# Attention forward and backward with a gated feed-forward block on one core: GpSimd's loads in program order, each tied to its own slot

## The chip, the core and the metric

The kernel runs on one core of a Trainium2 chip. The metric is the device time of one execution in microseconds (us); less is better. A core has five engines that run their own instruction streams: PE (TensorE), DVE (VectorE), ACT (ScalarE), POOL (GpSimd) and SP (SyncE). POOL and SP mostly issue transfers here, and the core's 16 DMA engines carry them. A GB/s is 10^9 bytes per second; a KB is 1024 bytes.

## The reference

From x (2048 x 576) comes xn = layernorm(x). Attention with 32 heads of width 128 takes its keys and values (2048 each) from caches; a second branch is a gated feed-forward block of inner width 4608. The output and the gradients for x, both caches and all weights are returned.

```python
xn = layernorm(x)
q = (xn @ wq) as 32 heads of 128
p = softmax(q @ k_cache^T * 128**-0.5)
s = (p @ v_cache, heads joined) @ wo
h = sigmoid(xn @ w_gate) * (xn @ w_up)
g = silu(h @ w_down)
out = x + s * g
# returned: out, and the gradients of A_x, A_k_cache, A_v_cache, A_wq, A_wo, B_w_gate, B_w_up, B_w_down for grad_out
```

## The kernel before

The work runs in stages: the feed-forward block forward (until about 490 us), attention forward and backward in one pass over the heads (490 to 3680 us), a first late stage that multiplies the heads' outputs by wo (3680 to 3830 us), and late stages for the remaining gradients.

*Attention* (function `attention(fast)`, L562). It is built twice, and a flag chooses the fast one, which is the one that ran. Its plan is written in slots, 2 x 16 for each of the 32 heads. In the first 16 slots of head h (from b1 = 32 h) the slot's `main1` makes a tile of 128 query rows: scores on PE (L600), exponential on ACT into a slab `Pq` of 128 x 2048 (L618), and a transpose of the slab by DMA from SP's queue (L594, `PT`). I call this the softmax phase. In the next 16 (from b2 = b1 + 16), the dp phase, `main2` makes dp = dO V^T on PE (L670) and multiplies it into the slab on DVE, the first half by way of ACT (L677, L678), the second half directly (L673); then the slab is transposed by DMA again (`dST`). Each slab is 512 KB, so each slot moves 512 KB through a DMA transpose. Five slots later (`skew`) the transposed tile is multiplied on PE (`tail1` with Vn, `tail2` with Kn, both L647), and every fourth slot a group of o or dq is stored by POOL (L641). The sums over queries for dV and dK (`Partial`, L706) run spread over eight slots each; every four steps L718 on DVE puts the result into a tile `kvo`, of which there are two buffers, and POOL stores it (L720): four stores of dV in the first half of the dp phase, four of dK in the first half of the next softmax phase.

*Other units of a slot.* `put(slot, cols, fn)` adds a unit of work to a slot; `plan(h)` puts all units of head h. For the next head it puts the loads of K and V in four parts of 128 KB (L178), wo (L172, L174) and wq (L164, L166), and their preparation: `prep_kt` (K transposed on PE, slot b2 + 8 of the head before), `prep_wot` and the four `prep_qt` (from b2 + 9), `prep_vt` (slot b1 + 6 of its own head). K and wq have two sets of buffers, V and wo one.

*Order.* In this stage no engine is held to the order in which the code is written: the Tile scheduler orders each engine's instructions, and a load goes into POOL's queue about as soon as its buffer is free. So the four V loads leave together when the last `tail1` of a head is done, and the four K loads when the last `tail2` of the head before is done. Each queue then runs in the order that was fixed: an instruction of POOL that waits holds up all behind it.

*Last head.* For the first late stage all of A_wo (4.7 MB) is loaded into buffers that the last head no longer needs (`wo_parts`, L535; `load_wo_rows`, L544), in parts of up to four heads (576 KB).

*First late stage* (from L860). For each of 16 row tiles, 32 x 2 matmuls (L902) multiply a transposed o tile `oT` (1 MB, DMA transpose from SP, L554; three buffers, loaded two tiles ahead) with wo. Then DVE combines the result with `dsg`, `g2b` and `xb`, which POOL loads for groups of SG1 = 2 tiles (288 KB each, L876), one group ahead, in two buffers each; POOL stores `xb` after each group (L912). SP and POOL are in program order there.

Of the kernel before, what the change touches and what calls it, by code (L numbers as in the profile page):

```python
# [9 lines left out]
bf = mybir.dt.bfloat16  # L10
# [3 lines left out]
P = 128  # L14
# [52 lines left out]
def kernel(  # L67
# [112 lines left out]
    def load_k(hs, c=0, n=1):  # L180
        load_kv(hs, hs.Kn, A_k_cache, c, n)
# [377 lines left out]
    NSC = S // CH  # L559
    nb = CH // P  # L560

    def attention(fast):  # L562
        with ExitStack() as es:
            def pool(name, bufs, **kw):
                return es.enter_context(tc.tile_pool(name=("f_" if fast else "g_") + name, bufs=bufs, **kw))
            slabp = pool("slab", SLABS)
# [123 lines left out]
            class Partial:  # L690
# [9 lines left out]
                def step(self):  # L700
                    kt = self.kt
                    j = kt % 4
                    if j == 0:
                        self.tile = acc_tile()
                    for qt in range(self.lo, self.hi):
                        nc.tensor.matmul(self.tile[:, j, :], lhsT=self.slabs[qt][:, kt * P:(kt + 1) * P], rhs=self.rhs[:, qt, :],  # L706
                                         start=(qt == self.lo), stop=(qt == self.hi - 1))
                    self.kt += 1
                    if j == 3 or self.kt == NT:
                        k0 = kt - j  # L710
                        if self.out_dram is None:
                            if self.factor == 1.0:
                                alt.copy(self.part[:, k0:kt + 1, :], self.tile[:, :j + 1, :], eng=self.eng)
                            else:
                                alt.scaled(self.part[:, k0:kt + 1, :], self.tile[:, :j + 1, :], self.factor, eng=self.eng)
                        else:
                            fo_ = stg.tile([P, 4, P], bf, name="kvo")
                            nc.vector.scalar_tensor_tensor(fo_[:, :j + 1, :], self.tile[:, :j + 1, :], self.factor, self.part[:, k0:kt + 1, :],  # L718
                                                           op0=ALU.mult, op1=ALU.add)
                            nc.gpsimd.dma_start(self.out_dram.rearrange("(p t) d -> p t d", t=NT)[:, k0:kt + 1, :], fo_[:, :j + 1, :])  # L720
# [7 lines left out]
            def put(slot, cols, fn):  # L728
                units.setdefault(slot, []).append((cols, fn))
# [18 lines left out]
            def q(k):  # L748
                return min(k, NT - 1)

            def plan(h):
                b1, b2 = 2 * NT * h, 2 * NT * h + NT
                hd = lambda: heads[h]
                pl = b2 - 2 * NT if h else None
                if h:
                    put(pl, 0, lambda: heads.__setitem__(h, start_head(h)))
                    for c in range(4):
                        put(pl + q(c), 0, lambda c=c: load_k(hd(), c, 4))
                        put(pl + q(skew + 3 + c), 0, lambda c=c: load_v(hd(), c, 4))
                    put(pl + q(4), 0, lambda: load_wo(hd()))  # L760
                    put(pl + q(5), 0, lambda: load_wq(hd()))
                    put(pl + q(skew + 3), NT * P, lambda: prep_kt(hd()))
                    put(pl + q(skew + 4), DT * P, lambda: prep_wot(hd()))
                    for sc in range(NSC):
                        put(pl + q(skew + 4 + 2 * sc), DT * CH, lambda sc=sc: prep_qt(hd(), sc))
                for qt in range(NT):
                    put(b1 + qt + skew, NT * P // 2, lambda qt=qt: tail1(hd(), qt, 0))
                    put(b1 + qt + skew, NT * P // 2, lambda qt=qt: tail1(hd(), qt, 1))
                for sc in range(NSC):
                    put(b1 + q(sc), DT * CH, lambda sc=sc: prep_dot(hd(), sc))  # L770
                    put(b1 + q(sc + 1), nb * P, lambda sc=sc: prep_don(hd(), sc))
                for qt in range(NT):
                    put(b1 + max(qt + 1, q(2 + qt // nb)), 0, lambda qt=qt: scale_don(hd(), qt))
                put(b1 + q(NSC + 2), NT * P, lambda: prep_vt(hd()))
                put(b1 + q(NTH + 2), NT * P, lambda: prep_qn(hd()))
                for qt in range(NT):
                    put(max(b1 + qt + 1, b1 + NT - 4 + qt // 2), 0, lambda qt=qt: scale_qn(hd(), qt))
                put(b2 + 1, 0, lambda: post1(hd()))
                parts = {}

                def first(key, rhs, lo, hi, eng, factor=1.0):
                    parts[key] = part_tile()
                    return Partial(hd(), lo, hi, rhs, parts[key], None, eng, factor)
                spread(b1 + NTH, lambda: first("v", hd().dOn, 0, NTH, "v"))
                spread(b2, lambda: Partial(hd(), NTH, NT, hd().dOn, parts["v"], out_3[0, h], None))
                spread(b2 + NTH, lambda: first("k", hd().Qn, 0, NTH, "s", SCALE))
                spread(b2 + NT, lambda: Partial(hd(), NTH, NT, hd().Qn, parts["k"], out_2[0, h], None, SCALE))
                for qt in range(NT):
                    put(b2 + qt + skew, NT * P // 2, lambda qt=qt: tail2(hd(), qt, 0))
                    put(b2 + qt + skew, NT * P // 2, lambda qt=qt: tail2(hd(), qt, 1))  # L790

            heads[0] = start_head(0)
            for h in range(H):
                plan(h)
            bl = 2 * NT * (H - 1) + NT
            for view, h0, n, dead in wo_parts:
                for k in range(0, n, 4):
                    at = (1 + k // 4, q(skew + 1), q(skew + 2), q(skew + 4), q(skew + 5))[dead]
                    put(bl + q(at), 0, lambda view=view, h0=h0, k=k, n=n: load_wo_rows(view, h0, k, min(k + 4, n)))
            for st in range(min(2, NT)):  # L800
                put(bl + NT + skew * st, 0, lambda st=st: load_oT(oTs[st], st))
            slot = 0
# [32 lines left out]
    with late("pc") as pc, late("pcw") as pcw, late("pcf") as pcf, \  # L835
# [21 lines left out]
                if i == DT - 1 and KPAD:  # L857
                    nc.gpsimd.memset(wdT_sb[:LO, i, r0:r0 + WCH], 0.0)

        with late("c1l3", 2) as ldp3, late("c1s", 2) as sb, \  # L860
                late("c1ps", 2, space=PSUM) as ps, late("c1pt", 2, space=PSUM) as pst:
            wo_of = {}
            for view, h0, n, _ in wo_parts:
# [2 lines left out]
            oTs.append(oT_view(xn_all[:].rearrange("p t d -> p (t d)"), 0))  # L866
            if NT > 2:
                load_oT(oTs[2], 2)
            SG1 = ldiv(NT, 2)
            NG1 = NT // SG1  # L870

            def group_loads(g):
# [4 lines left out]
                    res.append(t_)  # L877
                return res

            groups = {0: group_loads(0)}  # L880
            pend_tr = []
            for st in range(NT):
                if st and st + 2 < NT:
                    load_oT(oTs[(st + 2) % 3], st + 2)
                g, sl = divmod(st, SG1)
                if sl == 0:
                    if g + 1 < NG1:
                        groups[g + 1] = group_loads(g + 1)
                    dsg, g2b, xb = groups.pop(g)
                if st >= NT - 2 - DT and len(wd_pieces) > (F // WCH - 1) * DT:  # L890
                    wd_piece()
                if st == NT - NT // 4:
                    load_blk(ah0[:, 0, :, :], a_d, 0)
                    load_blk(ah0[:, 1, :, :], h_d, 0)
                while len(pend_tr) > 1:
                    st_ = pend_tr.pop(0)
                    transpose_to(nc, pst, doB[:, st_, :], D, doBT, st_ * P, ident, alt, eng="s")
                oT = oTs[st % 3]
                accs = [ps.tile([P, 512], f32, name=f"acc{j}") for j in range(len(ncs))]
                for h in range(H):  # L900
                    for j, (n0, nn) in enumerate(ncs):
                        nc.tensor.matmul(accs[j][:, :nn], lhsT=oT[:, h, :], rhs=wo_of[h][:, n0:n0 + nn],  # L902
                                         start=(h == 0), stop=(h == H - 1))
                s_sb = sb.tile([P, D], f32, name="s_sb")
                for j, (n0, nn) in enumerate(ncs):
                    alt.copy(s_sb[:, n0:n0 + nn], accs[j][:, :nn], eng="s")
                nc.vector.tensor_tensor(doB[:, st, :], s_sb[:], dsg[:, sl, :], op=ALU.mult)
                t0 = sb.tile([P, D], f32, name="t0")
                nc.vector.tensor_tensor(t0[:], s_sb[:], g2b[:, sl, :], op=ALU.mult)
                nc.vector.tensor_tensor(xb[:, sl, :], t0[:], xb[:, sl, :], op=ALU.add)  # L910
                if sl == SG1 - 1:
                    nc.gpsimd.dma_start(o0[g * SG1 * P:(g + 1) * SG1 * P, :].rearrange("(t p) d -> p t d", p=P), xb[:])  # L912
                pend_tr.append(st)
# [263 lines left out]
```

## Time and profile before

| what | value |
|---|---|
| three runs, median | 5086.49 us |
| lowest and highest of them | 5072.76 and 5111.36 us |
| the profiled execution: its own time | 5090.96 us |
| span of its instructions | 5089.0 us |
| mean granted TensorE clock | 0.993 |
| DMA issues of K and V parts | 128 KB, median 3.2 and 5.0 us to landing |
| DMA issues of dV and dK (kvo) | x256, 128 KB, median 4.2 us to landing |
| DMA transposes PT and dST | x512 each, median 4.9 and 5.2 us to landing |

A page of the profile gives each engine's busy time and its share of the span, then the chain of work that ended last, traced back from the last instruction: at each step to what released it. "issue" in it is time in which an engine waited for nothing that the profile shows. Groups and waits are named by line, engine and tiles (out<-in). A "landing" is the time from the issue of a transfer until its semaphore tells that it is done. DMA share is the mean busy share of the 16 DMA engines; it can exceed 1, since the packets of two queues overlap in the record.

### The profile page before, as it was taken

Reading aid. Unit: us, or ns where it says so; the run is one execution under the profiler, and the core shown is the slowest. Engines: PE = TensorE matmul, PEld = TensorE weight load, DVE = VectorE, ACT = ScalarE, POOL = GpSimd, SP = SyncE. Lnnn points to the kernel's source line nnn. Section 1 sums busy time; section 2 is a strip of 40 time slices with the busy share of each in tenths; the row PEclk is TensorE's granted clock in tenths of the full one; section 3 lists DMA queues with packets and bytes.
Section 4 is the critical chain, followed back from the end, with each engine's and each line's share of the span. In section 5 each row is a group of like instructions: output and inputs, shape, how many; then the busy total and the mean of one; then the engine's idle time right before and its main releaser. Section 6 shows DMA issues by size and latency. Waiting matters only on the chain.

```text
span 5089.0 us, 128042 instructions
## 1 busy us (share of the span) xinstructions
PE 4934.5 (97%) x53584; PEld 3485.5 (68%) x54480; DVE 2582.2 (51%) x6705; ACT 2577.3 (51%) x4636; POOL 938.9 (18%) x1449
## 2 busy tenths in 40 slices
PE   8999999999999999999999999999889999999999
PEld 4445777777787777778777777877646666555554
DVE  4544666666566666566666665666525444200111
ACT  5422666666676666667666666766413333211000
POOL 3322111111111111111111111111112222211000
PEclk9999999999999999999999999999999999999999
DMA  7776999999999999999999999999996665797976
GB/s 266 262 201 167 210 198 208 205 212 202 197 212 212 205 208 203 199 202 212 210 205 202 203 214 202 211 207 201 215 197 203 190 185 181 217 265 181 173 141 121
DMA packets 2762161, 1031.37 MB, mean 203 GB/s; under 512 B 2664737, under 2 KB 2668962, under 8 KB 2761570
## 3 DMA queue, kind: packets, MB, share of 16 engines
q1 hardware_dynamic: 2660354, 699.97, 74.0%
q0 software_dynamic: 101216, 323.05, 20.0%
q8 instruction: 428, 7.01, 0.6%
q14 instruction: 163, 1.34, 0.1%
HBM read 175.31 MB, written 182.13 MB: 70 GB/s over the span
## 4 chain that ended last, share of the span: by engine, by line
PE 83%; issue 8%; DMA 5%; DVE 1%; POOL 1%; ACT 1%; SPq 0%; POOLq 0%; DVEq 0%; ACTq 0%
PE acc L706 15%; PE acc L647 15%; PE acc L932 13%; PE sp L600 7%; PE acc L1103 7%; PE acc L213 5%; PE dp L670 5%; PE u_ps L420 3%; PE g_ps L418 3%; PE dh L985 3%; PE acct L146 2%; PE acc L503 2%; DMA out_dram<-kvo 2%; PE acc L902 2%; DVE Pq L673 1%
## 5 line engine op out<-in xcount | busy, mean ns | idle before, releaser
L618 ACT ACTIVATE Pq<-sp 128x1024 bf16<-128x1024 f32 x1024 | 1047.9, 1024 | 315.5 <-PE sp L600 202.1
L706 PEld LDWEIGHTS <-Pq 128*128 128x128 bf16 x16384 | 1006.9, 98 | 242.7 <-issue 5.0
L677 ACT ACTIVATE t<-dp,negdelta 128x1024 bf16<-128x1024 f32 x512 | 571.6, 1116 | 224.0 <-PE dp L670 170.6
L673 DVE SCALAR_TENSOR_TENSOR Pq<-dp,negdelta,Pq 128x1024 bf16<-128x1024 f32 x512 | 655.0, 1279 | 43.9 <-PE acc L647 41.1
L647 PEld LDWEIGHTS <-PT 128*128 128x128 bf16 x8192 | 503.1, 98 | 133.8 <-DMA PT<-Pq 13.3
L670 PE MATMUL dp<-VT,dOT 128*128 128x512 bf16 x1728 | 544.2, 382 | 36.6 <-DVE Pq L673 36.5
L647 PE MATMUL acc<-Vn,PT 128*128 128x128 bf16 x8192 | 548.3, 219 | 18.5 <-DMA PT<-Pq 11.6
L647 PE MATMUL acc<-Kn,dST 128*128 128x128 bf16 x8192 | 552.3, 219 | 8.5 <-DMA dST<-Pq 4.8
L706 PE MATMUL acc<-dOn,Pq 128*128 128x128 bf16 x8192 | 547.3, 219 | 10.1
L600 PE MATMUL sp<-KQ 128*128 128x512 bf16 x1762 | 547.5, 379 | 2.6 <-ACT Pq L618 2.5
L706 PE MATMUL acc<-Qn,Pq 128*128 128x128 bf16 x8192 | 544.7, 220 | 3.4
L647 PEld LDWEIGHTS <-dST 128*128 128x128 bf16 x8192 | 493.3, 98 | 67.4 <-DMA dST<-Pq 6.5
L678 DVE TENSOR_TENSOR Pq<-t,Pq 128x1024 bf16<-128x1024 bf16 x512 | 354.2, 692 | 358.3 <-ACT t L677 351.6
L687 ACT ACTIVATE dq_n<-acc,rsc 128x128 bf16<-128x128 f32 x512 | 188.3, 368 | 338.7 <-PE acc L647 338.7
L1119 DVE SCALAR_TENSOR_TENSOR junk<-acc,xn_all 128x512 f32<-128x512 f32 (+1 forms) x32 | 13.9, 453 | 640.7 <-ACT dxn L1118 640.7
L720 POOL DMA_DIRECT2D out_dram<-kvo x256 | 140.2, 548 | 1062.9 <-DVE kvo L718 1062.9
L641 POOL DMA_DIRECT2D on_d<-o_n x128 | 97.0, 758 | 741.5 <-DVE junk L659 390.0
L987 DVE TENSOR_TENSOR du_blk<-dh,ah 128x256 bf16<-128x256 f32 x288 | 120.1, 418 | 190.1 <-PE dh L985 188.0
L1118 ACT ACTIVATE dxn<-acc 128x512 f32<-128x512 f32 (+1 forms) x32 | 12.8, 407 | 397.8 <-PE acc L1103 390.3
L718 DVE SCALAR_TENSOR_TENSOR kvo<-acc,part 128x512 bf16<-128x512 f32 x256 | 175.9, 687 | 72.4 <-DMA out_dram<-kvo 38.8
L670 PEld LDWEIGHTS <-dOT 128*128 128x128 bf16 x2048 | 164.0, 98 | 64.4 <-issue 42.4
L605 DVE TENSOR_REDUCE rs_all<-rsp 128x1 f32<-128x2 f32 x512 | 78.0, 152 | 256.3 <-ACT Pq L618 254.1
(206 smaller groups left out, 6931.9 us busy)
## 6 DMA issues: line engine op xcount, KB each, us to landing
out_dram<-kvo POOLq DMA_DIRECT2D x256, 128.0 KB, 4.2
ah<-a_d POOLq DMA_DIRECT2D x18, 1024.0 KB, 7.2
ah<-h_d POOLq DMA_DIRECT2D x18, 1024.0 KB, 9.7
du_d<-du_blk POOLq DMA_DIRECT2D x18, 1024.0 KB, 8.6
dg_d<-dg_blk POOLq DMA_DIRECT2D x18, 1024.0 KB, 10.2
h_d<-h_row POOLq DMA_DIRECT2D x64, 256.0 KB, 3.2
x_all<-in_A_k_cache_dram SPq DMA_DIRECT2D x64, 256.0 KB, 3.8
a_d<-a_row POOLq DMA_DIRECT2D x64, 256.0 KB, 3.5
```

The costliest lines, as they stand in the source:

```text
L213: nc.tensor.matmul(av[:, :CH], lhsT=w[:, i, :], rhs=srcT[:, i, cs], start=(i == 0), stop=(i == DT - 1))
L600: nc.tensor.matmul(sp[:, c * CH:(c + 1) * CH], lhsT=hs.QT[:, qt * P:(qt + 1) * P], rhs=hs.KT[:, hf * HW_ + c * CH: hf * HW_ + (c + 1) * CH ...
L618: nc.scalar.activation(Pq[:, hsl], sp[:], AF.Exp, scale=SCALE, accum_out=hs.rsp[:, hf:hf + 1])
L647: nc.tensor.matmul(hs.acc[:, 0, :], lhsT=T[:, kt, :], rhs=rhs[:, kt, :], start=(kt == 0), stop=(kt == NT - 1))
L670: nc.tensor.matmul(dp[:, c * CH:(c + 1) * CH], lhsT=hs.dOT[:, qt * P:(qt + 1) * P], rhs=hs.VT[:, hf * HW_ + c * CH: hf * HW_ + (c + 1) * C ...
L673: nc.vector.scalar_tensor_tensor(Pq[:, hsl], dp[:], hs.negdelta[:, qt:qt + 1], Pq[:, hsl], op0=ALU.add, op1=ALU.mult)
L677: nc.scalar.activation(t[:], dp[:], AF.Identity, bias=hs.negdelta[:, qt:qt + 1], scale=1.0)
L678: nc.vector.tensor_tensor(Pq[:, hsl], t[:], Pq[:, hsl], op=ALU.mult)
L687: nc.scalar.activation(hs.dq_n[:, qt % G4, :], hs.acc[:, 0, :], AF.Copy, scale=hs.rsc[:, qt:qt + 1])
L706: nc.tensor.matmul(self.tile[:, j, :], lhsT=self.slabs[qt][:, kt * P:(kt + 1) * P], rhs=self.rhs[:, qt, :], start=(qt == self.lo), stop=(q ...
L932: nc.tensor.matmul(accs[j][:, :nn], lhsT=lhs[:, st, cols], rhs=rhs[:, st, n0:n0 + nn], start=(st == 0), stop=(st == NT - 1))
L1103: nc.tensor.matmul(self.accs[sl][j][:, :nn], lhsT=ch[:, kk, sl * P:(sl + 1) * P], rhs=wT[:, k0 + kk, n0:n0 + nn], start=(self.k + kk == 0) ...
```

## The change

In attention POOL's instructions keep the order in which the code writes them (`manual_schedule` for Pool). Each load of K, V, wq and wo for the next head, and each load of A_wo in the last head, moves to a slot of its own (`paced`), and ahead of it stands a GpSimd copy of one element of that slot's slab, so that POOL waits there until the first half of this slot's tile is written. K's parts go to slots b1 + 9, 10, 11 and 13 of the head before, wo to 14, wq to 15, V's parts to b2 + 9, 10, 11 and 13. A_wo is loaded in parts of two heads (288 KB) in slots that have no store (`free`), 18 loads in all, from slot b1 + 5 of the last head on. `kvo` gets four buffers. The scaling of Qn for the second half of the rows is put into later slots. In the first late stage the groups shrink from two row tiles to one, two groups are loaded ahead instead of one, and there are four buffers instead of two.

```diff
@@ attention @@
+    gate_t = pers.tile([1, 1], bf, name="gate_t")
     def attention(fast):
         with ExitStack() as es:
+            es.enter_context(tc.manual_schedule(engines={mybir.EngineType.Pool}))
...
-                            fo_ = stg.tile([P, 4, P], bf, name="kvo")
+                            fo_ = stg.tile([P, 4, P], bf, name="kvo", bufs=4)
...
+            def paced(slot, load):
+                def fn():
+                    if slot < 2 * NT * H:
+                        h, r = divmod(slot, 2 * NT)
+                        nc.gpsimd.tensor_copy(gate_t[:], heads[h].slabs[r % NT][0:1, 0:1])
+                    load()
+                put(slot, 0, fn)
...
                     for c in range(4):
-                        put(pl + q(c), 0, lambda c=c: load_k(hd(), c, 4))
-                        put(pl + q(skew + 3 + c), 0, lambda c=c: load_v(hd(), c, 4))
-                    put(pl + q(4), 0, lambda: load_wo(hd()))
-                    put(pl + q(5), 0, lambda: load_wq(hd()))
+                        paced(pl - NT + q((9, 10, 11, 13)[c]), lambda c=c: load_k(new_head(h), c, 4))
+                        paced(pl + q((9, 10, 11, 13)[c]), lambda c=c: load_v(hd(), c, 4))
+                    paced(pl - NT + q(14), lambda: load_wo(new_head(h)))
+                    paced(pl - NT + q(15), lambda: load_wq(new_head(h)))
...
-                    put(max(b1 + qt + 1, b1 + NT - 4 + qt // 2), 0, lambda qt=qt: scale_qn(hd(), qt))
+                    put(max(b1 + qt + 1, b1 + NT - 4 + qt // 2 if qt < NTH else b1 + NT + qt), 0, lambda qt=qt: scale_qn(hd(), qt))
...
+            dead_from = (5 - NT, 5 - NT, 9, 11, 4 - NT)
+            free = [k for k in range(5 - NT, NT + skew) if k not in (8 - NT, 12 - NT, 0, 1, 3, 4, 5, 7, 8, 12)]
             for view, h0, n, dead in wo_parts:
-                for k in range(0, n, 4):
-                    at = (1 + k // 4, q(skew + 1), q(skew + 2), q(skew + 4), q(skew + 5))[dead]
-                    put(bl + q(at), 0, lambda view=view, h0=h0, k=k, n=n: load_wo_rows(view, h0, k, min(k + 4, n)))
+                for k in range(0, n, 2):
+                    at = min([f for f in free if f >= dead_from[dead]] or [NT + skew])
+                    if at in free:
+                        free.remove(at)
+                    paced(bl + at, lambda view=view, h0=h0, k=k, n=n: load_wo_rows(view, h0, k, min(k + 2, n)))
@@ first late stage @@
-        with late("c1l3", 2) as ldp3, late("c1s", 2) as sb, \
+        with late("c1l3", 4) as ldp3, late("c1s", 2) as sb, \
...
-            SG1 = ldiv(NT, 2)
+            SG1 = 1
...
-            groups = {0: group_loads(0)}
+            groups = {g: group_loads(g) for g in range(min(2, NG1))}
...
-                    if g + 1 < NG1:
-                        groups[g + 1] = group_loads(g + 1)
+                    if g + 2 < NG1:
+                        groups[g + 2] = group_loads(g + 2)
```

In this plan pl is b2 of the head before, and bl is b2 of the last head.

## The prediction

> **What bounds the kernel now.** I read the page's busy shares and chain first.
>
> ```profile
> PE 4934.5 (97%) x53584; PEld 3485.5 (68%) x54480; DVE 2582.2 (51%) x6705; ACT 2577.3 (51%) x4636; POOL 938.9 (18%) x1449
> ...
> PE 83%; issue 8%; DMA 5%; DVE 1%; POOL 1%; ACT 1%; SPq 0%; POOLq 0%; DVEq 0%; ACTq 0%
> ```
>
> TensorE does all but 3% of the time, so a change to loads can win back only its stalls. To find these I took, from the trace, the start of each head's first multiply of L678: 31 periods, one per head. Fifteen of them are 97.68 or 97.69 us; that is the period without a stall, 3.05 us for each of 32 slots. The other sixteen are longer: heads 0-2, 7-10, 14-16, 21-23 and 28-29 are together 46.1 us over 97.68, and head 30 to 31 alone is 10.4 over. Windows over four such periods, then over what is left of attention, show it (columns: length, then busy us and count of PE, PEld, DVE, ACT, POOL; clock, DMA share, GB/s):
>
> ```profile
> 1821.97:1919.65 97.68, 96.39 (x1242) 77.51 (x1262) 62.23 (x164) 66.78 (x113) 17.08 (x28) 1.00 1.02 209
> 1919.65:2019.71 100.06, 96.72 (x1242) 77.55 (x1262) 62.28 (x164) 66.78 (x113) 17.11 (x28) 1.00 1.07 204
> 2121.68:2224.77 103.09, 98.19 (x1242) 78.84 (x1262) 62.38 (x165) 66.89 (x113) 17.11 (x28) 0.98 1.06 200
> 3508.73:3616.77 108.04, 98.34 (x1242) 78.49 (x1262) 62.27 (x165) 66.78 (x113) 18.37 (x28) 0.98 1.12 219
> 3616.77:3677.00 60.23, 53.58 (x728) 45.42 (x737) 35.32 (x49) 26.03 (x40) 9.37 (x14) 0.94 1.14 222
> ```
>
> The work is the same (x1242); only the length differs. Then the chain inside one long period, in order of time (start, us, what):
>
> ```profile
> 1929.55 0.53 POOL Vn L178
> 1930.08 0.01 issue
> 1930.09 0.49 POOL Vn L178
> 1930.58 0.04 issue
> 1930.62 0.51 POOL Vn L178
> ...
> 1933.20 8.37 DMA out_dram<-kvo
> ...
> 1941.69 0.10 DVE kvo L718
> 1941.79 0.51 issue
> 1942.30 1.28 DVE Pq L673
> 1943.58 0.04 issue
> 1943.62 0.38 PE dp L670
> ```
>
> Four V loads leave at once, as soon as the last tail1 has freed Vn. The dV store issued among them takes 8.37 us to land, against a median of 4.2 for these stores. kvo has two buffers, so the multiply L718 two stores later waits for that landing; VectorE is in order, so L673 waits behind it, the two score banks stay full, and TensorE's dp waits. In the fifteen clean heads the same store lands in 3.3 to 6.0 us and nothing waits; in the fifteen long ones up to head 29 in 6.3 to 10.5. The PE's waits from the last head to the end of the first late stage:
>
> ```profile
> PE acc L902 <- DMA KQ<-on_d: 15.1, 1, 15.1
> PE acc L647 <- DMA PT<-Pq: 11.6, 3, 4.8
> PE acc L902 <- DMA out_dram<-kvo: 2.6, 1, 2.6
> ```
>
> The 11.6 is the last head, where six transfers of A_wo, four of them of 576 KB, leave between 3571 and 3581 us; a probability transpose then takes 15.1 us to land instead of 4 to 6. The 15.1 is the first late stage: the transposed load of KQ, issued at 3689.3, takes 31.3 us while six group loads of 288 KB, then a store and two more loads, are in flight.
>
> **What the skill says.** "DMA: Bandwidth & Descriptors", Anatomy of one DMA: a semaphore wait happens on the issuing sequencer before dispatch, so a queue in program order holds everything behind a wait. The trace agrees: POOL sat 1062.9 us before dV and dK stores until their multiply was done. The same page, Queues, rings and completion order: a DMA engine alternates between queues packet by packet. That fits what is seen at 3690 to 3720 us, where transposes (256-byte packets) and bulk loads share the engines and both crawl. "SBUF — State Buffer", Who interferes with whom: a VectorE instruction with two SBUF inputs contends with a GpSimd instruction that reads SBUF; the new gate reads SBUF. Before has no such GpSimd read in attention, so no trace here shows it.
>
> **The change, part by part.**
> *Fast-path order.* In the compiled program PE, DVE, ACT and SP hold the same instructions in the same order in the fast branch; scale_qn's new slot changes nothing there, since the scheduler still fills VectorE with it early: 0 us. Only POOL's order, the waits and the late stage differ.
>
> *V loads.* They go from one burst at slots 3-4 of the dp phase to slots 9, 10, 11 and 13, behind the three dV stores instead of among them. Due: VT is made at slot 6 of the next head and the first tail1 at slot 5; the last load leaves at slot 13 and lands within 10 us by before's record (3 slots), so 5 slots (15 us) remain. K goes from a burst at slot 5 of the softmax phase to 9, 10, 11, 13, due at slot 8 of the dp phase; wo and wq at 14 and 15, due at slot 9. All have over 20 us.
>
> *kvo from 2 to 4 buffers.* L718 then waits for the store four back, which is over 35 us old at any of them; the longest landing of these stores in before was 10.5. Together these remove the long periods of heads 0-29. From both ends: 0, if the long landings come from something else, to -46.1. I take -46.
>
> *The gates.* 327 copies of one element, some 10 a head. Price: above a small VectorE operation (152 ns, L605) and below the GpSimd cast of 128x1152 (1.73 us); at 0.2 us a head costs POOL 2 us, on 17.1 busy of 97.7. Each waits for the first half of its own slot's tile; behind it on POOL stand this slot's load and the next o, dq and dV stores, which are due a slot or more later with 2 or 4 buffers. In exchange ACT and DVE get some 4 and 3 more wait instructions a head (17 ns each, by the one row of POOL's sequencer): 0.1 us, under ACT's 31 idle us a head. If the cover went, 327 x 0.2 = 65 us would show. I take 0.
>
> *Last head.* The 4.7 MB of A_wo now leave as 18 loads, 288 KB or less, one a slot, nine of them in slots 5-15 of the softmax phase. There transposes (512 KB a slot), loads and stores ask for about 8.8 MB in 33.5 us, 262 GB/s; slices of before moved 226 to 265 in this state. So a lag of some 5 us builds, plus two early transposed loads of 1 MB, and the skew of 5 slots (15.3 us less a landing of 5) hides 10. Lost now: 10.4, and 3.0 in its dp phase. Ends: -13 to 0. I take -9.
>
> *First late stage.* Loads become 144 KB, two groups ahead instead of one: nine loads (1.3 MB) go out before and during the KQ transpose instead of six (1.7 MB), then four transfers of 144 KB every 8.1 us row. The first burst is smaller, but POOL runs further ahead and the bytes beside that transpose hardly fall. 24 more loads and 8 more stores of 0.72 us are 23 us of POOL in a stage where it is idle: 0. Ends: -15 (wait gone) to +8 (more piled up). I take -5.
>
> Sum: -46 + 0 - 9 - 5 = -60. The profiled span of 5089.0 (5091.0 for the whole execution) becomes 5029; from the median of the runs, 5086.5, it is 5026.5.
>
> **The rivals.**
> *A, 55%:* as summed, 5026.5; its own range 5014 to 5042.
> *B, ends stay as they are, 22%:* the bytes at the end of attention and the start of the late stage hardly change, so those waits remain: 5086.5 - 46 = 5040. For it: the 262 GB/s above. Against: single loads of 288 KB before (3549.9 us) did not lengthen a transpose.
> *C, half, 10%:* the long periods come in groups seven heads apart, with the same bursts in every head. A beat that slows DMA itself would survive the move; only the deeper kvo would help: -23, 5063.
> *D, everything goes, 7%:* -46 - 13 - 15 - 2.6 = -77, 5009.
> *E, slower, 6%:* a load in each of ten slots mixes with the transposes. Need: 512 KB of transpose and 128 KB of load per 3.05 us, 215 GB/s. Ten lagging slots first use up the 10 us of skew; the gain of 60 is gone when each of 31 heads loses 1.9 us beyond that, so at 4.24 us a slot, 155 GB/s. Two slices of a K burst and of a V burst speak against it and for it (last column):
>
> ```profile
> 1890.00:1900.00 10.00, 9.89 (x141) 8.35 (x141) 6.27 (x27) 7.53 (x15) 1.84 (x3) 1.00 1.26 242
> 1930.00:1940.00 10.00, 9.90 (x136) 8.22 (x137) 7.81 (x11) 4.84 (x8) 3.53 (x7) 1.00 1.14 147
> ```
>
> At 147 a slot is 4.46 us: 14.1 - 10 = 4.1 us lost in each of 31 heads, 127 - 60 = +67, 5153. One load at a time should stay near the first slice.
>
> **How the numbers follow.** The range 5004 to 5062 holds A, B, D and the better half of C, and leaves out E, the rest of C and the tails. What a measurement of this kernel can tell from no change is about 1%, 51 us. Below 5035.6 lie D (0.07), most of A (0.48) and the lower edge of B (0.07), together 0.62; above 5137 most of E, 0.05; the rest, 0.33, lies between.
>
> **What would show it.** Right: all periods at 97.7, no kvo landing on the chain, L718 without a DMA wait, V loads alone on POOL. Wrong: a period over 99 (C, E), PE waiting for dST or PT in slots 9-15 (E), PT waits over 5 us in the last head or KQ over 12 (B), gates over 1 us each.

## The result and the profile after

| kernel | median of its runs | lowest to highest |
|---|---|---|
| before | 5084.65 us (4 runs) | 5072.76 to 5111.36 |
| after | 5260.54 us (4 runs) | 5228.26 to 5282.0 |

The ratio is 1.0333, with a 95% interval from 1.0265 to 1.0401: slower by 3.3%. The forecast was 5026.5 us, faster. The profiled execution of after has a span of 5285.6 us; it is another execution than the four timed ones and lies just above the slowest of them. The mean granted TensorE clock is 0.993 in both profiles, so the clock is not the reason.

First the busy times of after, and what its transfers took (for a queue: packets, MB, share of 16 engines' time).

```profile
PE 5019.8 (95%) x54480; PEld 3471.8 (66%) x54480; DVE 2589.2 (49%) x6705; ACT 2585.3 (49%) x4636; POOL 1014.8 (19%) x1816
...
q1 hardware_dynamic: 2660354, 699.97, 79.7%
```

The same row of before:

```profile
q1 hardware_dynamic: 2660354, 699.97, 74.0%
```

DVE and ACT have the same counts and nearly the same busy time (before: 2582.2 and 2577.3 us), so the gates slowed neither. PE's count differs from before (53584) because some of its records are missing from before's trace; PEld's is the same. What grew is SP's queue of transposes: the same packets and bytes took 79.7% x 5285.6 x 16 / 2660354 = 25.3 ns each on average instead of 74.0% x 5089.0 x 16 / 2660354 = 22.6. The median packet takes 18 ns in both traces; the mean grows because 7.1% of the packets take over 30 ns, where before 2.0% did.

Windows of after, over three periods of the heads and then over what is left of attention, as the prediction showed them for before:

```profile
2107.72:2213.05 105.33, 99.83 (x1263) 77.69 (x1262) 62.41 (x164) 67.15 (x113) 18.89 (x38) 0.98 1.14 194
2213.05:2317.25 104.20, 98.50 (x1263) 77.06 (x1262) 62.51 (x165) 67.00 (x113) 18.88 (x38) 1.00 1.17 194
2317.25:2418.25 101.00, 97.84 (x1256) 76.53 (x1255) 62.58 (x164) 66.97 (x112) 18.91 (x38) 1.00 1.14 202
3675.43:3789.28 113.85, 101.84 (x1280) 79.28 (x1281) 62.55 (x164) 67.14 (x113) 21.14 (x42) 0.99 1.15 208
3789.28:3858.00 68.72, 52.25 (x676) 42.31 (x674) 34.77 (x47) 25.47 (x38) 14.03 (x27) 0.95 1.14 212
```

No period is at 97.68 any more; all 31 last 101 to 114 us. POOL is busy 1.8 us more a head (ten gates), no more. PE's waits of after:

```profile
PE acc L650 <- DMA PT<-Pq: 126.2, 103, 5.8
PE acc L650 <- DMA dST<-Pq: 70.3, 69, 2.3
...
PE acc L917 <- DMA KQ<-on_d: 9.7, 3, 6.8
```

The wait of dp for DVE (36.5 us before) is gone, as forecast. In its place tail1 and tail2 (now L650) wait for the transposes: 196.5 us in 172 waits, some in every head, where before lost 16.4 in 10. The groups of the transposes show why. Before, then after (SP's instruction, duration ns min/median/max; landing in us):

```profile
L594 SPq DMA_TRANSPOSE PT<-Pq x512: 1417/2110/7821, 494.2 to 3624.7; - x171
...
DMA to landing us min/median/max: 3.6/4.9/15.1
```

```profile
L597 SPq DMA_TRANSPOSE PT<-Pq x512: 1479/3124/6205, 495.3 to 3799.0; - x171
...
DMA to landing us min/median/max: 4.3/6.4/12.6
```

Read the minimum first. The quickest transpose lands in 3.6 us before and none in under 4.3 after: they are slower by themselves, not only where loads stand beside them. SP's issue of one took 2.34 us on average before (heads 1 to 30, both kinds) and 3.17 after. The shortest issue hardly grew (1.42 to 1.48 us), so most of the mean looks like waiting behind earlier transposes. A head has 32 of them: 32 x 2.34 = 75 us fit into the clean period of 97.68; 32 x 3.17 = 101.4 don't. From head 1's dp phase to head 30's these issues fill 76% of SP's time before and 97% after: SP's queue had become what bounds a head.

Where the 196.6 us between the two profiled spans came in, by the starts of the dp phases: 4.4 before head 0's, 162.3 from there to head 30's, 5.8 to head 31's, 24.1 after it.

### The profile page after: what moved, and what is told of

Its sections match the earlier page's. It is cut to its first block, busy times and chain, and to the rows that moved or that the text cites. A ratio compares the mean times of both kernels' runs of the same rounds, so it can differ in the third digit from the quotient of the medians.

```text
span 5285.6 us, 129764 instructions
## 1 busy us (share of the span) xinstructions
PE 5019.8 (95%) x54480; PEld 3471.8 (66%) x54480; DVE 2589.2 (49%) x6705; ACT 2585.3 (49%) x4636; POOL 1014.8 (19%) x1816
## 3 DMA queue, kind: packets, MB, share of 16 engines
q1 hardware_dynamic: 2660354, 699.97, 79.7%
## 5 line engine op out<-in xcount | busy, mean ns | idle before, releaser
L650 PEld LDWEIGHTS <-PT 128*128 128x128 bf16 x8192 | 493.2, 98 | 290.5 <-DMA PT<-Pq 205.3
L650 PE MATMUL acc<-Vn,PT 128*128 128x128 bf16 x8192 | 551.8, 220 | 132.9 <-DMA PT<-Pq 126.2
L650 PE MATMUL acc<-Kn,dST 128*128 128x128 bf16 x8192 | 553.6, 219 | 72.5 <-DMA dST<-Pq 70.3
L673 PE MATMUL dp<-VT,dOT 128*128 128x512 bf16 x2048 | 613.3, 381 | 0.7 <-DVE Pq L676 0.5
L603 PE MATMUL sp<-KQ 128*128 128x512 bf16 x2048 | 609.7, 379 | 2.6 <-ACT Pq L621 2.5
L650 PEld LDWEIGHTS <-dST 128*128 128x128 bf16 x8192 | 488.5, 98 | 151.4 <-DMA dST<-Pq 99.4
L50 DVE TENSOR_SCALAR o_n<-acc,rinv_all 128x128 bf16<-128x128 f32 x352 | 123.2, 350 | 228.4 <-PE acc L650 228.3
L644 POOL DMA_DIRECT2D dq_d<-dq_n x128 | 97.5, 762 | 584.9 <-ACT dq_n L690 499.2
L621 ACT ACTIVATION_READ_ACCUMULATOR Pq<-sp 128x1 f32 x1024 | 200.5, 196 | 0.0
```

Of the source, the lines that this page charges most:

```text
L603: nc.tensor.matmul(sp[:, c * CH:(c + 1) * CH], lhsT=hs.QT[:, qt * P:(qt + 1) * P], rhs=hs.KT[:, hf * HW_ + c * CH: hf * HW_ + (c + 1) * CH ...
L621: nc.scalar.activation(Pq[:, hsl], sp[:], AF.Exp, scale=SCALE, accum_out=hs.rsp[:, hf:hf + 1])
L650: nc.tensor.matmul(hs.acc[:, 0, :], lhsT=T[:, kt, :], rhs=rhs[:, kt, :], start=(kt == 0), stop=(kt == NT - 1))
L673: nc.tensor.matmul(dp[:, c * CH:(c + 1) * CH], lhsT=hs.dOT[:, qt * P:(qt + 1) * P], rhs=hs.VT[:, hf * HW_ + c * CH: hf * HW_ + (c + 1) * C ...
```

## The experiments

**Theory 1: the place of the tiles.** The gate's target `gate_t` is a persistent tile of one element, allocated ahead of attention's tiles. In the compiled programs the first of the score slabs begins at byte 16896 of each SBUF partition before (33 x 512) and at 16928 after; the tiles behind it, the other slabs, PT and dST, kvo, and late blocks such as `du_blk`, move by the same 32 bytes. If a transfer from or to such an address is slower, every transpose is. **Theory 2:** the loads in slots 9 to 15 collide with the transposes (the prediction's rival E). **Theory 3:** the gates and POOL's program order cost by themselves.

*Before, moved by 32 bytes.*

```diff
+    gate_t = pers.tile([1, 1], bf, name="gate_t")
+    nc.gpsimd.memset(gate_t[:], 0.0)
```

> The kernel before, with one more persistent tile of a single element and one memset of it; no load, no wait and no order is touched. It moves the left side of SBUF by 32 bytes: the score slabs and the tiles that the DMA transposes write stand 32 bytes past a multiple of 512 instead of on one. Theory 1 (the address of the tiles slows every DMA packet): 5190 to 5260 us, SP's DMA transposes at about 3.2 us each in all slots instead of 2.3, head periods over 100 us. Theory 2 (the loads in slots 9 to 15 collide with the transposes) and theory 3 (the gates and the program order on GpSimd's queue): as the kernel before, 5070 to 5110 us, transposes at 2.3 us.

Measured: 5255.53 us, 1.0352 (1.0318 to 1.0386) of before. One tile of one element that nothing uses costs what the whole change costs.

```profile
PE acc L650 <- DMA dST<-Pq: 109.4, 72, 4.5
PE acc L650 <- DMA PT<-Pq: 77.5, 72, 8.2
```

*After, moved back.* The gate tile is 512 bytes wide; the gates still write one element.

```diff
-    gate_t = pers.tile([1, 1], bf, name="gate_t")
+    gate_t = pers.tile([1, 256], bf, name="gate_t")
-                        nc.gpsimd.tensor_copy(gate_t[:], heads[h].slabs[r % NT][0:1, 0:1])
+                        nc.gpsimd.tensor_copy(gate_t[0:1, 0:1], heads[h].slabs[r % NT][0:1, 0:1])
```

> The changed kernel with its gate tile made 512 bytes wide (the gates still write one element), so that every tile behind it stands on the same place in a block of 512 bytes as in the kernel before. All gates, the order and all loads stay. Theory 1 (address): about 5010 to 5040 us, as the forecast had the change itself, transposes at 2.3 us and all head periods near 97.7. Theory 2 (loads in slots 9 to 15 collide) and theory 3 (gates and order): 5240 to 5280 us as the changed kernel, periods of 101 to 108 us.

Measured: 5046.69 us, 0.993 (0.9903 to 0.9957) of before, 214 us under after. Three periods in its windows:

```profile
1901.12:1998.80 97.68, 96.39 (x1242) 77.48 (x1262) 62.24 (x164) 66.72 (x113) 18.88 (x38) 1.00 0.97 207
1998.80:2096.49 97.69, 96.40 (x1242) 77.51 (x1262) 62.26 (x165) 66.72 (x113) 18.88 (x38) 1.00 1.03 209
2096.49:2194.17 97.68, 96.39 (x1242) 77.49 (x1262) 62.24 (x165) 66.72 (x113) 18.87 (x38) 1.00 1.04 208
```

From head 1 to head 30 all 29 periods are 97.68 or 97.69, and head 0's is 97.86. With its loads in slots 9 to 15 and its gates, this kernel has no stall in attention until its last heads: theory 2 falls, and theory 3 as a cause of the loss.

*After without the gate copies* (the tile stays).

```diff
-                    if slot < 2 * NT * H:
-                        h, r = divmod(slot, 2 * NT)
-                        nc.gpsimd.tensor_copy(gate_t[:], heads[h].slabs[r % NT][0:1, 0:1])
```

> The changed kernel without the gate copies (the tile for them stays, so the addresses do too); program order on GpSimd's queue and all positions stay. Theory 1 (address) and theory 2 as far as positions hold without gates: 5220 to 5280 us. Theory 3 (the waits of the gates themselves cost): 5030 to 5090 us.

Measured: 5308.14 us, 1.0449 (1.0421 to 1.0476): slower than with the gates, which none of the three theories had foreseen. I return to it below.

*Both sides of SBUF on multiples of 512*: the kernel with the 512-byte gate tile, and 480 bytes of padding behind xnT on the right side.

```diff
+    pad_r = px.tile([P, 240], bf, name="pad_r")
+    nc.gpsimd.memset(pad_r[0:1, 0:1], 0.0)
```

> As the changed kernel with the 512-byte gate tile, and with 480 bytes of padding on the right side of SBUF, so that the normalised input, the o transposes' targets, K, V, dO and Q copies there stand on multiples of 512 too instead of 480 past one. Theory 1 (address): faster than with the left side alone, by up to 15 us where transposes into the right side are waited for (the last head and the start of the late stages), so 5000 to 5030 us. Theories 2 and 3: no change from the changed kernel, 5240 to 5280 us.

Measured: 5043.8 us, 0.9923 (0.9906 to 0.9941); not told apart from the 5046.69 without it, and outside the 5000 to 5030 that theory 1 had led me to expect.

**Which end of the transfer, and what multiple.** Two kernels move, in attention alone, either the slabs (source of the transposes) or PT and dST (destination); the padding behind puts all else back.

```diff
+            pad_a = pool("pad_a", 1).tile([P, 16], bf, name="pad_a")
             slabp = pool("slab", SLABS)
+            pad_b = pool("pad_b", 1).tile([P, 240], bf, name="pad_b")
```

> The kernel before, with 32 bytes of padding ahead of the score slabs and 480 behind them, in attention alone: only the slabs, which the DMA transposes read, stand off the multiple of 512; the tiles that they write stand on it. If the place of the source makes packets slow, 5190 to 5260 us; if that of the destination does, 5070 to 5100 us; if both cost, in between, near 5170 us.

```diff
             slabp = pool("slab", SLABS)
+            pad_a = pool("pad_a", 1).tile([P, 16], bf, name="pad_a")
...
             wpt = pool("wpt", 7 if fast else 4)
+            pad_b = pool("pad_b", 1).tile([P, 240], bf, name="pad_b")
```

> The kernel before, with 32 bytes of padding behind the slabs and 480 behind the transposed tiles, in attention alone: only the tiles that the DMA transposes write stand off the multiple of 512. If the place of the destination makes packets slow, 5190 to 5260 us; if that of the source does, 5070 to 5100 us.[...]

Measured: source moved 5239.93 us, 1.0312 (1.0274 to 1.035); destination moved 5082.34 us, 0.9998 (0.9984 to 1.0013). Before these runs I had thought the destination the likelier cause: wrong. The transposes' group with the source moved, then with the destination moved:

```profile
L598 SPq DMA_TRANSPOSE PT<-Pq x512: 1479/3052/12989, 495.1 to 3780.4; - x171
...
DMA to landing us min/median/max: 4.3/5.9/19.7
```

```profile
L598 SPq DMA_TRANSPOSE PT<-Pq x512: 1417/2120/7797, 494.1 to 3621.5; - x171
...
DMA to landing us min/median/max: 3.6/5.0/14.8
```

Three more kernels are before with a wider unused tile (`[1, 32]`, `[1, 64]`, `[1, 128]`: 64, 128 and 256 bytes).

> The kernel before with a persistent tile of 64 bytes, so everything on the left side stands 64 bytes past a multiple of 512. If what counts is a multiple of 64, as the kernel before, 5070 to 5100 us; if it is a multiple of 256 (the length of a packet) or of 128, 5190 to 5260 us.

> The kernel before with a persistent tile of 128 bytes: everything on the left side 128 bytes past a multiple of 512. If the slabs have to begin on a multiple of 256, the length of a transpose's packet, 5190 to 5260 us as with 32 and 64 bytes; if 128 is enough, 5070 to 5100 us as with 256.

> The kernel before with a persistent tile of 256 bytes, so everything on the left side stands 256 bytes past a multiple of 512. If what counts is a multiple of 256 or less, as the kernel before, 5070 to 5100 us; if it has to be a multiple of 512, 5190 to 5260 us.

| moved by | time | ratio to before (95%) | mean issue of a transpose (heads 1 to 30) |
|---|---|---|---|
| 32 bytes | 5255.53 us | 1.0352 (1.0318 to 1.0386) | 3.15 us |
| 64 bytes | 5256.28 us | 1.0365 (1.032 to 1.0409) | 3.13 us |
| 128 bytes | 5254.45 us | 1.0328 (1.0292 to 1.0365) | 3.15 us |
| 256 bytes | 5080.0 us | 0.9999 (0.9982 to 1.0015) | 2.40 us |

These four move source and destination together; the two kernels ahead of them put the cost on the source. So among the places tried the source has to stand on a multiple of 256 bytes, about the length of a packet here (699.97 MB in 2660354 packets, 263 bytes each on average). Last, the changed kernel with its one-element gate tile, all of it 32 bytes off but the slabs:

```diff
+            pad_a = pool("pad_a", 1).tile([P, 240], bf, name="pad_a")
             slabp = pool("slab", SLABS)
+            pad_b = pool("pad_b", 1).tile([P, 16], bf, name="pad_b")
```

> The changed kernel as it is, with its one-element gate tile and all other tiles 32 bytes off, but 480 bytes of padding ahead of the slabs in attention, so that the slabs alone stand on a multiple of 512. If the slabs as source are the whole of the loss, 5040 to 5055 us, as with the 512-byte gate tile (5046.7); if the other tiles' place carries part of it, 5060 us or more.

Measured: 5046.24 us, 0.9935 (0.9922 to 0.9948). The slabs' place is the whole of the loss.

**What the rest of the change is worth, with the slabs in place.** All of these start from the kernel with the 512-byte gate tile, but the last two, which start from before.

*The first late stage as before* (`SG1 = ldiv(NT, 2)`, two buffers, one group ahead).

> The changed kernel with the 512-byte gate tile and with the first late stage's loads as before (8 tiles in one load, 2 buffers). The forecast put the new late loads at -5 us, so 5050 to 5053 us here against 5046.7 with them; if the smaller loads bring nothing, 5045 to 5049 us. The wait for the first o transpose in the trace decides: 12 us or more if the large loads share its time, 7 us if they don't.

Measured: 5046.05 us, 0.9938 (0.9917 to 0.996), beside 5046.69 with the new loads: no gain shows. The interval, 11 us to each side, could still hide a few us. PE's wait for the first o transpose, which was to decide, is the same with the old loads and then with the new ones:

```profile
PE acc L917 <- DMA KQ<-on_d: 7.0, 1, 7.0
```

```profile
PE acc L917 <- DMA KQ<-on_d: 7.1, 1, 7.1
```

*The last head's A_wo loads as before* (four heads a load, at the slots of before, no gates).

> The changed kernel with the 512-byte gate tile and with the last head's A_wo loads as before: four heads in a load, at the places of before, without gates. The forecast put the new loads at -9 us, so 5054 to 5058 us here. If the split only moves the collision with the transposes of the last two heads (their waits sum to 21 us with it, 16.4 before), 5040 to 5048 us.

Measured: 5046.99 us, 0.994 (0.9919 to 0.9962): no gain shows here either, within the same 11 us. PE's waits with the old A_wo loads, and then with the new ones:

```profile
PE acc L650 <- DMA PT<-Pq: 11.6, 1, 11.6
...
PE acc L650 <- DMA dST<-Pq: 5.1, 3, 4.2
```

```profile
PE acc L650 <- DMA PT<-Pq: 11.1, 5, 7.3
PE acc L650 <- DMA dST<-Pq: 9.9, 4, 4.0
```

One long wait became several shorter ones.

*Without gates, program order kept.*

> The changed kernel with the 512-byte tile and without the gate copies: program order alone. If gates only hold a load where it would have been anyway, 5044 to 5050 us as with them. If program order alone lets the loads run ahead into the slots of the transposes (as the 48 us between the changed kernel with and without gates suggests), 5055 to 5095 us with periods over 98 us.

Measured: 5082.6 us, 1.0004 (0.9987 to 1.002): the gain is gone. Its profiled execution (span 5113.9 us) is its slowest of 14, so only the kind of wait is to be read from it:

```profile
PE acc L650 <- DMA PT<-Pq: 42.8, 18, 10.7
PE acc L914 <- DMA xn_all<-on_d: 25.0, 2, 23.7
```

At the end of head 30's softmax phase the last K part and the four loads of wo and wq leave between 3478.7 and 3481.0 us instead of in three slots, and the probability transpose issued among them, at 3479.8, takes 10.7 us to land. Of the 30 periods up to head 30, 14 are over 97.75 us; with the gates only head 0's was. So the gates are what spreads the loads; program order alone doesn't. The A_wo loads of the last head lose their gates here too, so how much of the loss is theirs is open.

*Before, with four output buffers and nothing else.*

```diff
-                            fo_ = stg.tile([P, 4, P], bf, name="kvo")
+                            fo_ = stg.tile([P, 4, P], bf, name="kvo", bufs=4)
```

> The kernel before with one edit: four output buffers for dV and dK instead of two. Loads and their order stay as before. If the long periods of before come from GpSimd waiting on an output buffer, most of the 41 us of attention's gain comes here: 5040 to 5055 us. If they come from the place of the V loads, which the four buffers leave alone, 5075 to 5090 us.

Measured: 5041.25 us, 0.9928 (0.9907 to 0.9949). This one edit gives all that the whole change gives with its slabs in place. In before, L718 on DVE sat idle until

```profile
  DMA out_dram<-kvo: 38.8, 15
  PE acc L706: 26.2, 36
```

and with four buffers only until

```profile
  PE acc L706: 26.1, 35
```

The landings of the stores (min/median/max), before and with four buffers, did not get shorter; L718 no longer waits for them. In the changed kernel with the 512-byte tile (third) they did:

```profile
DMA to landing us min/median/max: 2.0/4.2/10.5
```

```profile
DMA to landing us min/median/max: 2.0/4.4/20.2
```

```profile
DMA to landing us min/median/max: 2.0/3.4/7.9
```

*Four buffers and the right side on multiples of 512* (the padding shown above).

> The kernel before with four output buffers and 480 bytes of padding on the right side, so K, V, dO, Q and the o transposes' targets stand on a multiple of 512 too. Those are destinations of transposes and sources of none: if only a source's place counts, as with four buffers alone, 5038 to 5046 us; if a destination's place counts there, up to 10 us less.

Measured: 5045.21 us, 0.9926 (0.9896 to 0.9956): the place of destinations adds nothing here either. The versions from 5041 to 5047 us beat both kernels, by 0.6 to 0.8% of before, and are not told apart from each other; the single edit is the simplest of them.

## Why the prediction was wrong

**The step that failed** is the one that went "The gates. 327 copies of one element ... I take 0". It priced the copies and their waits, and not the tile that they write. The step above it, "Fast-path order", listed what differs between the two programs ("Only POOL's order, the waits and the late stage differ") after comparing instructions, not addresses: every tile on the left side had moved by 32 bytes. The copies did cost about nothing (1.8 us of POOL a head, hidden, as estimated: 2). The tile cost 214 us: 5260.54 with one element, 5046.69 with 512 bytes. In before the same 32 bytes cost 173 us (5255.53 against 5082.76). As I read it, the 41 us between the two are the gain that four buffers can't bring where SP's queue sets the pace: from head 0's dp phase to head 30's, before moved by 32 bytes takes 3124.7 us, and after, with its four buffers, 3139.1. No rival, either, let a transpose be slower by itself; E slowed it only through its neighbours.

**Why a multiple of 256.** The Trainium skill's page "DMA: Bandwidth & Descriptors", How a descriptor splits into AXI transactions, says that a transaction must start at an address that is a multiple of 256 bytes, so that a descriptor which begins elsewhere has its first transaction start at the boundary below. By that rule a 256-byte row off the multiple takes two transactions instead of one. The runs agree on the multiple (128 slow, 256 not), and they show the cost on the reading side. By that page's beats of 32 bytes such a row would cost 9 beats at 32 bytes off and 12 at 128, an estimate; the runs show no growth with the offset (3.15, 3.13, 3.15 us), so if this is the cause, the number of transactions counts here. No trace shows transactions, and the median packet took 18 ns in both kernels, so the mechanism inside the DMA engine stays open; that the slabs' place costs the time is shown. The same page, DMA Transpose, Constraints, asks for 32-byte alignment in SBUF: the slabs of after met that and were slow.

**V loads and kvo, -46:** right in size and place, wrong in its share. From head 0's dp phase to head 30's, before took 2976.8 us and the kernel with the 512-byte tile 2930.7: -46.1. But the move of the V loads was not needed for it: before with four buffers alone took 2931.3, -45.5. The edit that ends the wait was enough, without the one that was to shorten the landing. That one did shorten it (longest 10.5 to 7.9 us); whether it would have been enough alone was not run.

**Gates at 0:** wrong in a second way. Against before they cost nothing, but program order without them loses 36 us (5082.6 against 5046.69); with the slabs misplaced, 48 us (5308.14 against 5260.54).

**Last head, -9, and first late stage, -5:** neither shows, though intervals of 11 us to each side can't exclude them. The remaining balance of the two spans is +1.4 us ahead of attention, +3.6 in the last period and +1.8 after it; with the -46.1 that makes -39.3, the difference of the spans. Both estimates rested on single waits of one execution. The 15.1 us wait for KQ was anything from 2.7 to 15.2 us in the eight other kernels whose first late stage was untouched: 2.7 moved by 32 bytes, 6.3 with the destination moved, 8.2 with four buffers, 15.2 with the source moved. A wait that varies so much is no base for -5.

**The rivals.** B (5040: the ends stay) describes the kernel with the slabs in place, 5046.69. C falls: four buffers took all of the gain, not half, and no slow beat of DMA outlived the move of the loads (longest landing 7.9 us). Why the long periods of before come in groups seven heads apart stays open. E came nearest to the time (5153) and named the right symptom, PE waiting for dST and PT, with the wrong cause: with the slabs in place the same loads in the same slots stop nothing up to head 30.

## What to carry over

A new tile, however small, can move all that is allocated behind it: after an edit compare addresses as well as instructions, and keep tiles that transposes read at a multiple of 256 bytes. When a profile shows the same transfers of a queue taking longer everywhere, even at their minimum, look for what changed in the transfer itself before blaming its neighbours. When a wait sits on too few buffers, try the buffers alone first.

## What was not expected of the hardware

- A DMA transpose of 512 KB from SBUF takes some 3.15 us of SP's issue on average in this kernel instead of 2.34 when its source stands 32, 64 or 128 bytes past a multiple of 256; its shortest landing goes from 3.6 to some 4.3 us. With its destination alone 32 bytes off no cost shows (0.9998, 0.9984 to 1.0013).
- Plain stores of 1 MB from SBUF show it mildly. With their blocks 32 bytes off (after with the slabs put right), and then on a multiple of 512 (the 512-byte gate tile), issue to landing:

```profile
du_d<-du_blk POOLq DMA_DIRECT2D x18, 1024.0 KB, 9.7
dg_d<-dg_blk POOLq DMA_DIRECT2D x18, 1024.0 KB, 11.6
```

```profile
du_d<-du_blk POOLq DMA_DIRECT2D x18, 1024.0 KB, 8.7
dg_d<-dg_blk POOLq DMA_DIRECT2D x18, 1024.0 KB, 10.3
```

  The shortest landing of `du_d` is 7.1 us in all six kernels whose block is 32, 64 or 128 bytes off, and 5.4 in all others. The times of the two kernels are not told apart (5046.24 and 5046.69 us), so this is hidden here.
- Of two ways to hold a load back, a queue's program order and a copy that waits for a tile, only the second spread the loads over slots; the difference was 36 us. Neither is needed here: before's own order with four buffers takes 5041.25 us.
